# Attention and FFN on one core: v with keys on partitions, and a 32-bit path through TensorE transposes for the first four attention jobs

## The chip, the core and the metric

The kernel runs on one core of one Trainium2 chip. The time is the device time of one launch in microseconds (us). A profile is one execution of the same program under the hardware profiler.

The engines are called as in the profile: PE is TensorE's matrix product and PEld its weight load, DVE is VectorE, ACT is ScalarE, POOL is GpSimd and SP is SyncE, which here only issues transfers. ACT issues some transfers too (ACTq in the profile).

## The reference

There are 8 batches of 8 heads, 576 positions and a head dimension of 64. The attention is causal, with a bias from running sums of a per-position value; its output, with the heads side by side, goes through a feed-forward network (FFN) with a piecewise activation.

```python
scores = scale * np.matmul(q, k.transpose(0, 1, 3, 2))
cum = np.cumsum(np.maximum(s, 0.0), axis=-1)
bias = -(cum[:, :, :, None] - cum[:, :, None, :])
scores = np.where(causal, -1000000000.0, scores + np.minimum(bias, 0.0))
attn = np.exp(scores - np.max(scores, axis=-1, keepdims=True))
attn = attn / (np.sum(attn, axis=-1, keepdims=True) + 1e-09)
out = np.matmul(attn, v)                       # 8 x 8 x 576 x 64
x = out.transpose(0, 2, 1, 3).reshape(8 * 576, 512)
h = x @ w_in                                   # 512 x 2048
g = np.where(h >= 1, h, np.where(h <= -1, 0.0, (h + 1) ** 2 / 4))
result = g @ w_out                             # 2048 x 512
```

q, k, v and s are 32-bit floating point; w_in and w_out come in 64 bits.

## The kernel before

**Split numbers.** Large products run in 16-bit floats on TensorE, but each operand is held as a high half and a low half (the rest after rounding), each scaled by a power of two or by a bound of the largest value. A product of two such operands takes three TensorE passes: high by high, low by high and high by low.

**Attention jobs.** A job is a pair of heads (n, from 0 to 31) and a half of the queries (hf). The first half has 320 queries in three tiles of 64, 128 and 128; the second has 256 in two tiles. The list `jobs` (L492) runs through the first halves of a batch's four pairs, then through its second halves. A job has eight slots (`att_slot`, L494): slot 0 loads the running sums' rows, slots 2 to 7 issue one unit of scores each, slot 3 loads the next job's q and k, and slot 7 issues the attention product of the job before.

For a unit, `scores` (L393) multiplies q by k on PE (L408 in 32 bits for the first twelve jobs, later L411 and L412), adds the mask and takes the row minimum of the negated scores on DVE (L417), and takes the exponential with its row sums on ACT (L428). When both heads of a tile are done, `weights_t` (L434) makes the weights: DVE forms 1/sum (L444, L445), POOL writes the first head's high half (L449), ACT scales the second head in place (L450), POOL writes that one's high and low half (L451, L452), and DVE writes the first head's low half (L455, in `rest`). Then SP transposes the tile by DMA (L456) from `pb` into `pt`, since the product needs the keys on partitions. `att_out` (L463) runs the three-pass product of `pt` and `vt` on PE (L474), 18 instructions for a first half and 30 for a second, and writes x in two halves on ACT (L485) and DVE (L486).

**v.** `load_v` (L253) brings a batch's v, transposed on the host, with the two heads' dimensions on partitions and 576 keys along the row. `batch_v` and `batch_scales_v` (L258, L267) take its largest value for every partition (L262), a power of two for each, and one maximum over all partitions by a PE transpose and a spread (`column_max`, L107, and `spread`, L117). `v_prep` (L365) clears the pad (L371) and writes the high half on POOL (L372); for the first four pairs POOL also scales v and writes the low half (L374, L375), for the others DVE writes it in `v_turn` (L382). `v_turn` then transposes the tile by DMA (L384).

**Weights.** The first stage of the program decodes w_in from 64-bit words in 16 chunks of 128 x 512, four to each of the first four jobs: ACT takes absolute values (L200) and, for every second chunk, decodes a low part (L207); DVE takes the chunk's peak (L201) and joins the bits (L202, L208, or L210 and L211). After all chunks `w1.scale` (L213) forms the bound of the weight: a maximum over the peaks (L216), a PE transpose of it (L107), small DVE steps, a spread through PE (L117), and the reciprocal (L223, L224). With it, `split` (L226) writes the halves: ACT the high half (L229), and DVE (L237) or POOL (L232, L235) the low half. The transfers of w_out also wait for that bound. The second stage decodes and splits w_out in the same way, between the first FFN steps.

**FFN.** For each 128 of the 2048 inner columns, `ffn_h` (L521) runs twelve products (L528), and ACT and DVE form the activation (L540, L543, L544); ACT and POOL split it (L554, L555), and `ffn_y` (L559) multiplies by w_out (L567). Each batch's halves are 16 such steps. The first half of the first batch runs all its `ffn_h` before its `ffn_y`, since w_out isn't ready.

**Order.** The code issues instructions in program order under a planner that simulates a time line and puts each engine's instructions in an order by it; a `tc.high_priority(offset=...)` block moves its instructions ahead by the offset, and `tc.issue_after` holds one behind another. On the chip each engine's queue runs in the order written. The first stage reads:

```python
load_v(0)
batch_start(0)
for j in range(NPAIR):
    for k in range(8):
        if k % 2 == 0:
            c = 4 * j + k // 2
            w1.decode(c)
            w1.load(c + 3)
        att_slot(j, k)
while late:
    late.pop(0)()
w1.scale(0, LEAST_A)
```

Of the kernel before, what the change touches and what calls it, by code (L numbers as in the profile page):

```python
# [27 lines left out]
SP = NB * P  # L28

# [18 lines left out]
W2_LEAD = 6000  # L48

# [10 lines left out]
F32_JOBS = 12  # L60
V_POOL = 4
# [12 lines left out]
def attention_ffn(ctx: ExitStack, tc: tile.TileContext, qT, kT, vT, s, w_in, w_out, yT):  # L74
# [183 lines left out]
    def batch_v(b):  # L258
        c = csc[b] = ap.tile([P, NPAIR], F32, tag="csc", name=f"c{b}")
        r = rcs[b] = ap.tile([P, NPAIR], F32, tag="rcs", name=f"rc{b}")  # L260
        for p in range(NPAIR):
            V.tensor_reduce(c[:, p:p + 1], vraw[b, p], axis=AX, op=ALU.max, apply_absolute_value=True)  # L262
        pow2floor(c, c, TINY)
        V.reciprocal(r, c)
        V.tensor_scalar(r, r, 4096.0, None, ALU.mult)
# [99 lines left out]
    def v_prep(n):  # L365

        b, p = n // NPAIR, n % NPAIR
        v = vraw.pop((b, p))
        r = rcs[b][:, p:p + 1]
        VB = ap.tile([P, 2, SP], F16, tag="vb", bufs=1, name=f"vb{n}")  # L370
        G.memset(VB[:, :, S:], 0.0)  # L371
        G.tensor_scalar(VB[:, 0, :S], v, r, 1.0, ALU.mult, ALU.mult)  # L372
        if n < V_POOL:
            G.tensor_scalar(v, v, r, 1.0, ALU.mult, ALU.mult)  # L374
            G.tensor_tensor(VB[:, 1, :S], v, VB[:, 0, :S], ALU.subtract)  # L375
        vbs[n] = VB, v, r

    def v_turn(n):
        VB, v, r = vbs.pop(n)
        if n >= V_POOL:  # L380
            with tc.issue_after(ttr[0]):
                V.scalar_tensor_tensor(VB[:, 1, :S], v, r, VB[:, 0, :S], ALU.mult, ALU.subtract)  # L382
        VT = vts[n] = ap.tile([P, 2 * NB, P], F16, tag="vt", bufs=5, name=f"vt{n}")
        nc.sync.dma_start_transpose(out=VT, in_=VB.rearrange("p l n -> p (l n)"))  # L384

# [47 lines left out]

    def weights_t(n, i):  # L434
# [3 lines left out]
        h_off, N, tiles = HALF[hf]  # L438
        if i == tiles[0]:
# [23 lines left out]
    def att_out(n, hf):  # L463
# [19 lines left out]
        e = exs[b][:, p:p + 1]  # L483
# [10 lines left out]
    def att_slot(j, k):  # L494

        if j < len(jobs):
# [11 lines left out]
            if k == 1 and j % (2 * NPAIR) == V_J and j // (2 * NPAIR) + 1 < B:  # L508
# [101 lines left out]
    batch_scales(0)  # L610
# [77 lines left out]
```

## Time and profile before

| | |
|---|---|
| time, median of 3 runs | 1112.76 us (1111.5 to 1112.82) |
| time of the profiled execution | 1112.3 us |
| its span, first to last instruction | 1110.2 us |
| mean granted PE clock | 0.982 |
| bytes moved by DMA | 153.70 MB |
| DMA transposes `pt` and `vt` | 160 and 32 |

The page cuts the span into 40 slices and shows for each engine the busy share in tenths. A table of stretches gives, for each stretch, the microseconds that each engine was busy, the number of its instructions, the granted PE clock (1.00 is full), the share of time in which the DMA engines were busy, and GB/s. A group line reads: line of the kernel, engine, operation, output and input, shape, count, then busy time in us and the mean of one in ns, then the idle time before the group's instructions and what ended it. A line of one source line gives minimum, median and maximum ns, and the first and last start.

### The profile page before, as it was taken

How to read it: one execution, taken by the hardware profiler on the slowest of the kernel's cores; microseconds unless marked ns; L12 is line 12 of the kernel's file. 1: busy time of each engine (PE TensorE's matmuls, PEld its weight loads, DVE VectorE, ACT ScalarE, POOL GpSimd, SP SyncE). 2: the span in 40 equal slices, each digit the busy share in tenths (PEclk: the TensorE clock that was granted, in tenths of full speed). 3: DMA queues.
4: the chain of work that ended last, by engine and by line, in shares of the span. 5: the costliest groups of instructions: out<-in, count | busy, mean ns of one | idle time of the engine just before them, and what ended most of it. 6: DMA issues, size and time to landing. Idle time of an engine off the chain costs nothing.

```text
span 1110.2 us, 25043 instructions
## 1 busy us (share of the span) xinstructions
PE 999.0 (90%) x8470; PEld 771.2 (69%) x8470; DVE 855.0 (77%) x2392; ACT 715.9 (64%) x1683; POOL 657.2 (59%) x1161
## 2 busy tenths in 40 slices
PE   0454799899999999999999999999999999899998
PEld 0132466588767877777777877787777877787787
DVE  7979987578868877878787877787777886887533
ACT  3647766467557775777567775877576755777432
POOL 3666275676647664766566755766476665765522
PEclk9997899699999999999999999999999999999999
DMA  8984536767638763987558763977387874666300
GB/s 257 241 174 129 186 78 126 140 120 152 127 84 187 165 151 72 181 164 158 106 119 186 156 149 74 193 155 167 68 178 155 170 129 80 152 156 138 68 24 20
DMA packets 339623, 153.70 MB, mean 138 GB/s; under 512 B 290728, under 2 KB 321320, under 8 KB 339496
## 3 DMA queue, kind: packets, MB, share of 16 engines
q1 hardware_dynamic: 329792, 142.17, 60.2%
q10 hardware_dynamic: 9704, 9.93, 2.9%
q8 instruction: 67, 1.10, 0.4%
q14 instruction: 60, 0.49, 0.1%
HBM read 71.00 MB, written 9.73 MB: 73 GB/s over the span
## 4 chain that ended last, share of the span: by engine, by line
PE 61%; DVE 15%; DMA 7%; POOL 7%; issue 6%; ACT 4%; ACTq 0%; DVEq 0%; SPq 0%; POOLq 0%
PE h L528 25%; PE y L567 24%; PE px L474 4%; DMA pt<-pb 4%; PE s L411 3%; DVE pb L455 3%; PE s L412 3%; DVE p L417 2%; POOL pb L449 2%; DVE Q1s L362 1%; ACT u L540 1%; PE s L408 1%; DMA wor<-in_moe_w_out_dram 1%; POOL pb L452 1%; DVE h L543 1%
## 5 line engine op out<-in xcount | busy, mean ns | idle before, releaser
L528 PE MATMUL h<-x,WI 128*128 128x256 f16 (+1 forms) x3072 | 463.5, 290 | 22.2 <-DVE u L544 19.6
L567 PE MATMUL y<-g,WO 128*128 128x256 f16 (+1 forms) x3072 | 453.0, 287 | 8.4 <-POOL g L555 6.5
L528 PEld LDWEIGHTS <-WI 128*128 128x128 f16 x3072 | 291.2, 99 | 116.3 <-issue 27.9
L567 PEld LDWEIGHTS <-WO 128*128 128x128 f16 x3072 | 288.1, 98 | 93.4 <-issue 13.8
L555 POOL TENSOR_TENSOR g<-u,g 128x320 f16<-128x320 f32 (+1 forms) x256 | 204.5, 799 | 161.2 <-ACT g L554 156.1
L428 ACT ACTIVATE p<-p,mn 64x64 f32<-64x64 f32 (+4 forms) x320 | 179.5, 561 | 140.2 <-DVE mn L417 123.0
L540 ACT ACTIVATE u<-h,ub,us 128x320 f32<-128x320 f32 (+1 forms) x256 | 149.3, 583 | 121.6 <-PE h L528 119.7
L543 DVE SCALAR_TENSOR_TENSOR h<-h,ws,u 128x320 f32<-128x320 f32 (+1 forms) x256 | 132.4, 517 | 96.9 <-ACT u L540 94.4
L449 POOL TENSOR_SCALAR pb<-p,rs 64x128 f16<-64x128 f32 (+4 forms) x160 | 95.3, 595 | 173.3 <-DVE rs L445 108.0
L452 POOL TENSOR_TENSOR pb<-p,pb 64x128 f16<-64x128 f32 (+4 forms) x160 | 169.1, 1057 | 9.3
L455 DVE SCALAR_TENSOR_TENSOR pb<-p,rs,pb 64x128 f16<-64x128 f32 (+4 forms) x160 | 132.3, 827 | 44.9 <-POOL pb L449 44.7
L417 DVE CUSTOM_DVE_ANT_0 p<-s,mask 64x64 f32<-64x64 f32 (+4 forms) x320 | 134.6, 421 | 33.5 <-PE s L412 17.4
L544 DVE SCALAR_TENSOR_TENSOR u<-u,r,h 128x320 f32<-128x320 f32 (+1 forms) x256 | 130.2, 509 | 6.2
L411 PE MATMUL s<-K1s,Q1s 128*128 128x288 f32 (+4 forms) x312 | 117.5, 378 | 11.4 <-DVE Q1s L362 7.1
L450 ACT ACTIVATE p<-p,rs 64x64 f32<-64x64 f32 (+4 forms) x160 | 89.5, 559 | 58.9 <-DVE rs L445 57.7
L554 ACT CAST g<-u 128x320 f16<-128x320 f32 (+1 forms) x256 | 108.1, 422 | 9.8 <-DVE u L544 9.1
L451 POOL TENSOR_SCALAR pb<-p 64x128 f16<-64x128 f32 (+4 forms) x160 | 93.9, 587 | 11.8 <-ACT p L450 10.0
L412 PE MATMUL s<-K2s,Q2s 68*128 68x288 f32 (+4 forms) x312 | 95.9, 307 | 1.1 <-DMA K2s<-cumd 0.7
L474 PEld LDWEIGHTS <-vt 128*64 128x64 f16 x1536 | 74.0, 115 | 32.9 <-issue 17.9
L474 PE MATMUL px<-pt,vt 128*64 128x256 f16 (+3 forms) x1536 | 84.1, 262 | 10.8 <-DMA pt<-pb 6.8
L411 PEld LDWEIGHTS s<-K1s,Q1s 128*128 128x128 f32 (+1 forms) x312 | 56.6, 181 | 21.2 <-issue 6.7
L363 DVE TENSOR_TENSOR K2s<-rk,K1s 64x1152 fp32r<-64x1152 f32 (+1 forms) x52 | 59.1, 1136 | 2.2 <-ACT K1s L360 0.9
(123 smaller groups left out, 963.3 us busy)
## 6 DMA issues: line engine op xcount, KB each, us to landing
rk<-in_k_dram SPq DMA_DIRECT2D x56, 288.0 KB
v<-in_v_dram SPq DMA_DIRECT2D x32, 288.0 KB
wir<-in_moe_w_in_dram SPq DMA_DIRECT2D x16, 512.0 KB
wor<-in_moe_w_out_dram SPq DMA_DIRECT2D x16, 512.0 KB
rk<-in_k_dram SPq DMA_DIRECT2D x48, 160.0 KB
rq<-in_q_dram SPq DMA_DIRECT2D x48, 160.0 KB
rq<-in_q_dram SPq DMA_DIRECT2D x56, 128.0 KB
out_dram<-o ACTq DMA_DIRECT2D x32, 160.0 KB
```

Source lines behind the costliest of these rows:

```text
L411: T.matmul(sc[:R, :c1 - c0], Q1[:, hd, qo:qo + R], K1[:, hd, c0:c1], start=True, stop=False)
L417: ttr[0] = V.tensor_tensor_reduce(out=Pt[:R, c0:c1], in0=sc[:R, :c1 - c0], in1=mask[:R, mo:mo + c1 - c0], scale=-0.125, scalar=3.0e38 if m ...
L428: A.activation(Pt[:R, :W], Pt[:R, :W], AF.Exp, bias=m2[:R], scale=-1.0, accum_out=sums[n, i][:R, hd:hd + 1])
L452: G.tensor_tensor(los[1], pw, his[1], ALU.subtract)
L455: V.scalar_tensor_tensor(los[0], pv, rs[:R, :1], his[0], ALU.mult, ALU.subtract)
L474: T.matmul(px[hd * D:(hd + 1) * D, lo:N], VT[:, vl * NB + j, hd * D:(hd + 1) * D], PT[:, 4 * j + 2 * hd + pl, lo:], start=(m == 0), stop=( ...
L528: T.matmul(h[:, :N], WI[4 * kt + ft // 4][:, wl, ft % 4 * P:(ft % 4 + 1) * P], x[:, kt, xl], start=(n == 0), stop=(n == 3 * NKT - 1),)
L540: first = A.activation(u, h[:, :N], AF.Relu, bias=ubi[b], scale=usc[b]).ins
L543: V.scalar_tensor_tensor(h[:, :N], h[:, :N], wsc[b], u, ALU.mult, ALU.max)
L544: V.scalar_tensor_tensor(u, u, r, h[:, :N], ALU.min, ALU.mult)
L555: G.tensor_tensor(g[:, 1], u, g[:, 0], ALU.subtract)
L567: T.matmul(ys[b, hf, m][:, :N], WO[8 * (m // 2) + ft // 2][:, wl, c0:c0 + P], g[:, gl], start=(ft == 0 and n == 0), stop=(ft == NFT - 1 an ...
```

## The change

v comes from the host with keys in rows and a pair's two heads side by side; a tile holds 128 keys on partitions and five blocks of keys along the row, the last one half filled and cleared on POOL. So `vt` is written in place by `v_prep` and `v_low`, over 640 columns, and v's DMA transposes go. v has one scale for a batch instead of one for each partition. Each load is two transfers.

The first four jobs (`PLAIN_JOBS`) take another path, `plain_t`: POOL normalizes both heads' weights in place in 32 bits, PE transposes them in blocks of up to 128 keys into the PSUM banks that the FFN's second product uses later, ACT copies them into a 32-bit `pt`, and PE multiplies them by v as loaded, in 32 bits. v's halves for the first four pairs are prepared in jobs 4 and 5, for the second halves of the queries. The next batch's v is loaded one job later in the first batch.

v's load and its scale move into the first job (slots 2 and 6), and `w1.scale` and `batch_scales(0)` get a lead of 6000 in the planner.

```diff
     def load_v(b):
         for p in range(NPAIR):
-            v = vraw[b, p] = ap.tile([P, S], F32, tag="vraw", bufs=4, name=f"v{b}_{p}")
-            nc.sync.dma_start(v, vT[b, p])
+            v = vraw[b, p] = ap.tile([P, NB, P], F32, tag="vraw", bufs=4, name=f"v{b}_{p}")
+            G.memset(v[TAIL:, NB - 1], 0.0)
+            nc.sync.dma_start(v[:, :NB - 1], vn[b, p, :SP - P].rearrange("(j p) n -> p j n", p=P))
+            nc.sync.dma_start(v[:TAIL, NB - 1], vn[b, p, SP - P:])
...
     def v_prep(n):
...
-        VB = ap.tile([P, 2, SP], F16, tag="vb", bufs=1, name=f"vb{n}")
-        G.memset(VB[:, :, S:], 0.0)
-        G.tensor_scalar(VB[:, 0, :S], v, r, 1.0, ALU.mult, ALU.mult)
+        VT = vts[n] = ap.tile([P, 2, NB, P], F16, tag="vt", bufs=5, name=f"vt{n}")
+        G.tensor_scalar(VT[:, 0], v, r, 1.0, ALU.mult, ALU.mult)
         if n < V_POOL:
             G.tensor_scalar(v, v, r, 1.0, ALU.mult, ALU.mult)
-            G.tensor_tensor(VB[:, 1, :S], v, VB[:, 0, :S], ALU.subtract)
+            G.tensor_tensor(VT[:, 1], v, VT[:, 0], ALU.subtract)
...
-        nc.sync.dma_start_transpose(out=VT, in_=VB.rearrange("p l n -> p (l n)"))
...
+    def plain_t(n, i):
...
+        V.tensor_scalar(rs[:R], sums.pop((n, i))[:R], EPS, 2.0 ** -12, ALU.add, ALU.mult)
+        V.reciprocal(rs[:R], rs[:R])
+        for hd, Pt in enumerate(pbs.pop((n, i))):
+            G.tensor_scalar(Pt[:R, :W], Pt[:R, :W], rs[:R, hd:hd + 1], 1.0, ALU.mult, ALU.mult)
+            pp = ps_y.tile([P, 512], F32, tag=f"y{turn[0] % 4}", name=f"pp{n}_{i}_{hd}")
+            turn[0] += 1
+            for j in range(i + 1):
+                T.transpose(pp[:, j * R:(j + 1) * R], Pt[:R, j * P:(j + 1) * P], ident[:R, :R])
+            A.copy(
+                PT[:, hd:2 * (i + 1):2, off - h_off:off - h_off + R],
+                pp[:, :(i + 1) * R].rearrange("p (j r) -> p j r", r=R),
+            )
...
     def att_out(n, hf):
...
+        if plain(n, hf):
+            e = exs[b]
+            for j in range(nj):
+                lo = max(0, j * P - h_off)
+                for hd in range(2):
+                    T.matmul(
+                        px[hd * D:(hd + 1) * D, lo:N], vraw[b, p][:, j, hd * D:(hd + 1) * D],
+                        PT[:, 2 * j + hd, lo:], start=(j == 0), stop=(j == nj - 1),
+                    )
...
-            if k == 1 and hf == 0:
+            if plain(n, 0):
+                if k in (1, 4) and hf == 1 and j < PLAIN_JOBS + 2:
+                    v_prep(2 * (j - PLAIN_JOBS) + k // 4)
+            elif hf == 0 and k == 1:
                 v_prep(n)
-            if k == V_K and hf == 0:
-                v_turn(n)
+            elif hf == 0 and k == V_K:
+                v_low(n)
...
-    load_v(0)
-    batch_start(0)
     for j in range(NPAIR):
         for k in range(8):
...
+            if (j, k) == (0, 2):
+                load_v(0)
+            if (j, k) == (0, 6):
+                batch_start(0)
             att_slot(j, k)
     while late:
         late.pop(0)()
-    w1.scale(0, LEAST_A)
-    batch_scales(0)
+    with tc.high_priority(offset=SCALE_LEAD):
+        w1.scale(0, LEAST_A)
+        batch_scales(0)
```

More of the change, by code (lines that the diff above doesn't have):

```diff
@@ L48 @@
 W2_LEAD = 6000
+SCALE_LEAD = 6000
 G_BUFS = 4
@@ L60 @@
 F32_JOBS = 12
+PLAIN_JOBS = 4
 V_POOL = 4
@@ L73, in attention_ffn @@
 @with_exitstack
-def attention_ffn(ctx: ExitStack, tc: tile.TileContext, qT, kT, vT, s, w_in, w_out, yT):
+def attention_ffn(ctx: ExitStack, tc: tile.TileContext, qT, kT, vn, s, w_in, w_out, yT):
     nc = tc.nc
@@ L315, in whole, with plain @@
         return jobs.index((n, hf)) < F32_JOBS
+    def plain(n, hf):
+        return jobs.index((n, hf)) < PLAIN_JOBS
     def operands(n, hf):
@@ L367, in v_prep, with v_low @@
         b, p = n // NPAIR, n % NPAIR
[L368 to L372 removed]
+        v, r = vraw.pop((b, p)), rcs[b]
+        VT = vts[n] = ap.tile([P, 2, NB, P], F16, tag="vt", bufs=5, name=f"vt{n}")
+        G.tensor_scalar(VT[:, 0], v, r, 1.0, ALU.mult, ALU.mult)
         if n < V_POOL:
             G.tensor_scalar(v, v, r, 1.0, ALU.mult, ALU.mult)
[L375 to L379, printed above, removed]
+            G.tensor_tensor(VT[:, 1], v, VT[:, 0], ALU.subtract)
+        vbs[n] = VT, v, r
+    def v_low(n):
+        VT, v, r = vbs.pop(n)
         if n >= V_POOL:
             with tc.issue_after(ttr[0]):
[L382 to L384 removed]
+                V.scalar_tensor_tensor(VT[:, 1], v, r, VT[:, 0], ALU.mult, ALU.subtract)
     vbs = {}
@@ L432, in scores @@
             weights_t(n, i)
+    def plain_t(n, i):
+        off, R, W = QT[i]
+        h_off, N, tiles = HALF[i // 3]
+        if i == tiles[0]:
+            pts_[n, i // 3] = ap.tile([P, 2 * (tiles[-1] + 1), N], F32, tag="pt", bufs=2, name=f"pt{n}_{i // 3}")
+        PT = pts_[n, i // 3]
+        rs = ap.tile([P, 2], F32, tag="rs", bufs=4, name=f"rs{n}_{i}")
+        V.tensor_scalar(rs[:R], sums.pop((n, i))[:R], EPS, 2.0 ** -12, ALU.add, ALU.mult)
[10 more added lines that the diff above has]
+            )
+    turn = [0]
     def weights_t(n, i):
@@ L438, in weights_t @@
         h_off, N, tiles = HALF[hf]
+        if plain(n, hf):
+            plain_t(n, i)
+            return
         if i == tiles[0]:
@@ L467, in att_out @@
         nj = tiles[-1] + 1
-        PT, VT = pts_.pop((n, hf)), vts[n]
+        PT, e = pts_.pop((n, hf)), 2.0 ** -12
         px = ps_s.tile([P, 512], F32, tag="s", name=f"px{n}_{hf}")
-        steps = [(j, vl, pl) for j in range(nj) for vl, pl in ((0, 0), (1, 0), (0, 1))]
+        if plain(n, hf):
+            e = exs[b]
[6 more added lines that the diff above has]
+                    )
+        steps = [] if plain(n, hf) else [(j, vl, pl) for j in range(nj) for vl, pl in ((0, 0), (1, 0), (0, 1))]
         for m, (j, vl, pl) in enumerate(steps):
@@ L507, in att_slot @@
                 att_load(*jobs[j + 1])
-            if k == 1 and j % (2 * NPAIR) == V_J and j // (2 * NPAIR) + 1 < B:
+            if k == 1 and j % (2 * NPAIR) == V_J + (j < 2 * NPAIR) and j // (2 * NPAIR) + 1 < B:
                 load_v(j // (2 * NPAIR) + 1)
@@ L670 @@
         "in_k_dram": c(inputs["k"].transpose(0, 1, 3, 2)),
-        "in_v_dram": c(inputs["v"].transpose(0, 1, 3, 2)).reshape(B, NPAIR, P, S),
+        "in_v_dram": c(inputs["v"].reshape(B, NPAIR, 2, S, D).transpose(0, 1, 3, 2, 4)).reshape(B, NPAIR, S, P),
         "in_s_dram": c(inputs["s"]).reshape(B * H, S),
```

33 lines of the change are left out of this document (14 added, 19 removed).

## The prediction

> **What bounds the kernel now.** I read the page first, for who is busy when.
>
> ```profile
> span 1110.2 us, 25043 instructions
> PE 999.0 (90%) x8470; PEld 771.2 (69%) x8470; DVE 855.0 (77%) x2392; ACT 715.9 (64%) x1683; POOL 657.2 (59%) x1161
> ...
> PE   0454799899999999999999999999999999899998
> ...
> DVE  7979987578868877878787877787777886887533
> ```
>
> TensorE holds the last six sevenths; before that, VectorE is the full engine. The change works on the beginning, so the table of stretches is cut there: 24.3 is the first score product, 63.8 the end of the last w_in peak, 84.9 the third pair's turn in the first FFN product, 160 the place where TensorE fills.
>
> ```profile
> core 0: us, PE busy (x) PEld busy (x) DVE busy (x) ACT busy (x) POOL busy (x), PEclk, DMA share, GB/s
> 0.00:24.30 24.30, 0.51 (x2) 0.18 (x2) 16.02 (x39) 9.13 (x10) 6.92 (x19) 1.00 0.83 255
> 24.30:63.80 39.50, 17.62 (x55) 9.04 (x54) 36.83 (x112) 24.07 (x58) 27.13 (x49) 1.00 0.99 233
> 63.80:84.90 21.10, 11.44 (x73) 7.54 (x74) 15.79 (x61) 10.23 (x27) 9.97 (x27) 1.00 0.81 180
> 84.90:160.00 75.10, 51.23 (x284) 31.21 (x284) 69.80 (x161) 55.00 (x96) 42.68 (x43) 0.86 0.45 133
> ...
> 210.00:1050.00 840.00, 818.27 (x7257) 645.42 (x7257) 661.81 (x1865) 569.17 (x1383) 525.59 (x954) 1.00 0.67 140
> ```
>
> Up to 160 us VectorE works 138.4 us (the sum of four rows) and is idle 21.6: 8.3, 2.7, 5.3 and 5.3. From 210 to 1050 TensorE is idle only 21.7 of 840. So a microsecond that leaves VectorE's path before 160 moves the end by about one; later it moves nothing. DMA is the second suspect: its share is 0.99 from 24 to 64. The third is a position in a queue:
>
> ```profile
> 63.68 0.15 DVE L216 TENSOR_REDUCE t_wi<-peak_wi 128x1 f32<-128x16 f32 x1
> ...
> 76.50 0.37 PE L107 MATMUL row_wi<-ident,t_wi 128*1 128x128 f32 x1
> ...
> 80.76 0.14 DVE L224 TENSOR_SCALAR r_wi<-r_wi 128x1 f32<-128x1 f32 x1
> ```
>
> The first weight's largest value stands at 63.8, TensorE takes it up at 76.5, and its reciprocal, for which every w_in split waits, is there at 80.9: 17.1 us for about 3 us of small steps.
>
> **VectorE's ledger, the terms of the sum.** Groups of VectorE from 0 to 81 us, then the spread of four of them (minimum/median/maximum ns; L211's rows from the whole span):
>
> ```profile
> L417 DVE CUSTOM_DVE_ANT_0 p<-s,mask 64x64 f32<-64x64 f32 (+2 forms) x24 | 8.3, 345 | 2.6 <-POOL pb L452 1.5 <-PE s L408 1.1
> L202 DVE TENSOR_SCALAR WO<-WO 128x512 int32<-128x512 int32 x16 | 8.0, 501 | 0.1
> L455 DVE SCALAR_TENSOR_TENSOR pb<-p,rs,pb 64x128 f16<-64x128 f32 (+2 forms) x12 | 8.0, 664 | 4.2 <-POOL pb L449 4.2
> L208 DVE SCALAR_TENSOR_TENSOR WO<-wir,WO 128x512 int32<-128x512 int32 x8 | 7.7, 962 | 0.3 <-ACT wir L207 0.3
> L211 DVE SCALAR_TENSOR_TENSOR WO<-wir,WO 128x512 int32<-128x512 int32 x8 | 6.8, 856 | 0.0
> L444 DVE TENSOR_SCALAR rs<-sm 128x2 f32<-128x2 f32 (+1 forms) x12 | 4.3, 360 | 0.4 <-ACT p L428 0.4
> L262 DVE TENSOR_REDUCE c<-v 128x1 f32<-128x576 f32 x4 | 3.0, 750 | 1.3 <-DMA v<-in_v_dram 1.3
> ```
>
> ```profile
> L202 DVE TENSOR_SCALAR WO<-WO x16: 404/414/1292, 8.5 to 63.1; 128x512 int32<-128x512 int32 x16
> L208 DVE SCALAR_TENSOR_TENSOR WO<-wir,WO x8: 659/682/2489, 9.7 to 56.6; 128x512 int32<-128x512 int32 x8
> L211 DVE SCALAR_TENSOR_TENSOR WO<-wir,WO x8: 675/686/1595, 13.4 to 65.4; 128x512 int32<-128x512 int32 x8
> L444 DVE TENSOR_SCALAR rs<-sm x160: 150/169/1111, 30.1 to 1037.4; 128x2 f32<-128x2 f32 x128, 64x2 f32<-64x2 f32 x32
> ```
>
> 1. Four plain jobs have no low half of the weights, so 12 of L455 go: **-8.0** of work, and with them the 4.2 idle that waited on GpSimd's L449: **-4.2**.
> 2. v's four reductions no longer stand first in the queue; the 1.3 us wait for v goes: **-1.3**. They read 640 instead of 576 columns: 3.0 x 64/576 = **+0.3**. The other steps on v's scale are the same small ones in another order: nothing.
> 3. Mean against median of four groups: 16 x 0.087 + 8 x 0.280 + 8 x 0.170 + 12 x 0.191 = 7.3 us by which VectorE's instructions are stretched. I put that down to GpSimd running beside them: it works 44.0 us up to 84.9, so 0.166 per GpSimd microsecond (bounds: nothing, if the cause is another, or all of it). What GpSimd loses and gets:
>
> ```profile
> L452 POOL TENSOR_TENSOR pb<-p,pb 64x128 f16<-64x128 f32 (+2 forms) x12 | 9.5, 788 | 0.4
> L449 POOL TENSOR_SCALAR pb<-p,rs 64x128 f16<-64x128 f32 (+2 forms) x12 | 7.1, 593 | 16.0 <-DMA pt<-pb 4.9 <-DVE rs L444 4.8 <-issue 2.9
> L451 POOL TENSOR_SCALAR pb<-p 64x128 f16<-64x128 f32 (+2 forms) x12 | 6.6, 549 | 0.7 <-ACT p L450 0.7
> L375 POOL TENSOR_TENSOR vb<-v,vb 128x576 f16<-128x576 f32 x4 | 5.4, 1351 | 0.1
> L372 POOL TENSOR_SCALAR vb<-v,rc 128x576 f16<-128x576 f32 x4 | 4.0, 1004 | 16.7 <-DVE rc L265 16.7
> L374 POOL TENSOR_SCALAR v<-v,rc 128x576 f32<-128x576 f32 x4 | 3.0, 738 | 0.1
> ```
>
> L449, L451 and L452 go for 12 tiles: 23.2. v's preparation (L372, L374, L375, 12.4) moves to jobs 4 and 5, behind 84.9. Added are 24 normalizations f32 to f32 of 64, 192 and 320 columns. By L374 (738 ns for 576 columns) they cost 8 x 0.74 = 5.9, by L449's mean 24 x 0.593 = 14.2; I take 8, since L374 has the same types. GpSimd falls by 27.6 us, and VectorE's stretch by 27.6 x 0.166 = **-4.6**.
> 4. The moved 12.4, at 640 columns 13.8, now lies in the stretch from 84.9 to 160, where VectorE is 93% busy: 13.8 x 0.166 = **+2.3** (bounds 0 and 13.8, each GpSimd microsecond stopping VectorE wholly).
>
> Work: -8.0 + 0.3 - 4.6 + 2.3 = -10.0. Idle: -5.5. Together **-15.5**.
>
> The largest row bears on a rule. L208's worst took 2489 ns against 682. The Trainium skill, SBUF — State Buffer, section Who interferes with whom, says that VectorE and GpSimd share one pair of ports, held for a whole instruction, so that the second of two such instructions waits fully. The 2489 ns agrees; by that rule the moved preparation could cost its full length, and that is rival D.
>
> **What is added elsewhere and why it stays covered.**
>
> ```profile
> L408 PE MATMUL s<-K2w,Q2w 68*64 68x64 f32 (+2 forms) x24 | 10.8, 573 | 14.0 <-DVE mn L417 11.3 <-issue 2.6
> ...
> L107 PE MATMUL row_m<-ident,mt x8: 270/273/372, 23.0 to 917.0; 128*1 128x128 f32 x8
> ...
> L408 PEld LDWEIGHTS s<-K2w,Q2w x72: 132/192/338, 35.2 to 242.4; 68*128 68x128 f32 x56, 68*64 68x64 f32 x16
> ...
> L428 ACT ACTIVATE p<-p,mn 64x64 f32<-64x64 f32 (+2 forms) x24 | 10.8, 449 | 11.4 <-DVE mn L417 5.8 <-DVE rs L445 4.8 <-POOL p L403 0.7
> L450 ACT ACTIVATE p<-p,rs 64x64 f32<-64x64 f32 (+2 forms) x12 | 5.3, 442 | 4.8 <-DVE rs L445 4.8
> ```
>
> TensorE gets 48 transposes of 128 columns in 32 bits (2, 4 and 6 per job for the three tiles). By L107 alone each costs 0.27, by L107 plus a 32-bit weight load up to 0.27 + 0.34: 13 to 29 us; I take 16, since loads overlap products. The product in 32 bits has 6 instructions instead of 18; between nothing and +2 us per job, I take nothing. TensorE then works some 46 of the first 85 us instead of 29.6, covered while VectorE is the fuller. ACT gets 24 copies out of PSUM of 64 to 384 columns, 24 x 0.45 = 10.8 by L428 and L450, and loses L450's 5.3: 49 of 85.
>
> The DMA queues lose in this part 12 transposes of weights and 4 of v (by their shapes 2.9 + 1.3 = 4.2 MB; the first three stretches moved 19.2 MB, so a fifth). SP carries no transposes any more that hold back w_in loads. v's rows become 512 bytes long in two transfers each, which may cost more than now; the freed fifth covers that. I count nothing for DMA, up or down; what it could give is rival C. The later 28 transposes of v lie where TensorE sets the time: nothing.
>
> The bound's lead brings splits and w_out loads nearer to 64 us. I don't count it on top: VectorE must still do its ledger before 160; the lead is what lets it do so without the idle time of item 1 coming back as a wait for the bound. Late next is then the last job's tail and ACT's splits, which before stood behind 80.9.
>
> The profiled execution took 1112.3 us, 2.1 outside its span: 1112.3 - 15.5 = 1096.8. The median of the three runs is 0.5 higher, so I say **1097**.
>
> **The rivals.** About 0.2%, 2.2 us, is what a measurement of this kernel can tell from no change.
>
> - **B, work without idle.** The 5.5 us of waits return in another form (a product waits for its copy, the bound's small steps wait in VectorE's queue). For it: every hop through TensorE and ACT is in order. Then -10.0, 1103; without relief from GpSimd (item 3 at nothing) -8.0 + 0.3 + 2.3 = -5.4, 1107.
> - **C, DMA was the limit too.** For it: share 0.99. The early idle of 8.3 loses 3 more, TensorE's 21.7 later loses a fifth, 4, as v's transposes leave SP's queue: -22.5, 1090. Against: VectorE was 93% busy in that very stretch.
> - **D, the moved v preparation stops VectorE for its full 13.8** instead of 2.3: 11.5 more, 1109. Against: the mean stretch is a sixth of GpSimd's time.
> - **E, slower: transposes serialize the attention.** TensorE's queue is in order; if each tile's transposes stand ahead of the next tile's scores, a tile costs its whole chain: two scores 1.15, mask and minimum 0.35, exponential 0.45 and its sum, rs 0.36, two normalizations 0.67, four transposes 1.1, a copy 0.45: 4.6, and with three hops that wait behind a 0.5 us VectorE instruction 6.1. Twelve tiles: 73 us from 24.3, and 3 for the last product, so the FFN begins at 100 instead of 84.9: +15, 1128. It decides from 5.0 us per tile, where 24.3 + 60 + 3 passes 84.9 by 2.2. Against: two score buffers and four p buffers let the next scores go ahead. The Trainium skill, TensorE: Matmul & The Clock Gate, Part 4, adds that transposes don't count as activity for the clock, so that TensorE might run slow there; here the granted clock is 1.00 in all stretches to 84.9 and no row shows a run of transposes.
> - **F, no change.** The copies stand in ACT's queue ahead of w_in's first decode step, and each of 16 chunks starts 1 us later (a transpose group, 1.1): 16 us, which cancels the gain: 1112.
>
> **How the numbers follow.** A, the forecast, 0.46 (own range 1092 to 1102); B 0.18; C 0.14; D 0.06; F 0.06; E 0.10. Faster is A to D, 0.84; same 0.06; slower 0.10. The range leaves out F and E and reaches from C with a margin, 1087, to D, 1109.
>
> **What would show it.** VectorE's busy time up to the filling of TensorE near 128 us; L455 absent before the fifth job; r_wi within 5 us of t_wi; the FFN's first product near 70; TensorE full from about 145, and the stretch of 840 us as long as now. Wrong, if r_wi comes early but TensorE fills at 155 or later (B, D or F: look for waits on transposes in ACT and for stretched L202 behind 84.9), if the scores of job 3 end later than now (E), or if the later stretch shortens by over 3 us (C).

## The result and the profile after

The changed kernel takes **1120.14 us** (median of seven runs, 1115.6 to 1121.97) against 1112.76 (seven runs, 1109.08 to 1115.96): ratio 1.0059, 95% interval 1.0034 to 1.0084, so slower by some 7 us. The prediction was 1097. The profiled execution took 1121.97 us.

The page of the changed kernel, in the lines that stand ahead of the prediction for the kernel before:

```profile
span 1120.2 us, 24958 instructions
...
PE 1018.8 (91%) x8494; PEld 777.5 (69%) x8494; DVE 844.7 (75%) x2364; ACT 716.5 (64%) x1695; POOL 676.0 (60%) x1149
...
PE   2584699899999999899999999999999999999998
...
DVE  6759897678777877787778877887778877887533
```

The table of stretches of the changed kernel, cut at the same times as before:

```profile
core 0: us, PE busy (x) PEld busy (x) DVE busy (x) ACT busy (x) POOL busy (x), PEclk, DMA share, GB/s
0.00:24.30 24.30, 3.41 (x10) 1.83 (x10) 18.13 (x48) 10.02 (x17) 7.91 (x23) 1.00 0.82 231
24.30:63.80 39.50, 24.09 (x71) 12.84 (x73) 28.96 (x96) 23.61 (x59) 16.01 (x37) 1.00 0.71 177
63.80:84.90 21.10, 18.98 (x77) 10.74 (x74) 9.04 (x46) 13.03 (x34) 9.82 (x24) 0.68 0.38 115
84.90:160.00 75.10, 47.07 (x248) 28.51 (x248) 69.35 (x154) 49.86 (x86) 37.84 (x42) 0.77 0.43 125
...
210.00:1050.00 840.00, 816.36 (x7208) 640.26 (x7205) 656.34 (x1855) 567.70 (x1384) 551.39 (x952) 0.99 0.62 129
```

VectorE works 125.5 us up to 160 (four rows) instead of 138.4. Only part of these 13 us is work that left: at 160 the changed kernel is also less far (12 steps of u done, 15 in the kernel before). Up to 84.9 VectorE is idle for 28.8 us (6.2, 10.5 and 12.1) instead of 16.3. In 63.8 to 84.9, TensorE is the full engine: 19.0 of 21.1 us.

Where VectorE's idle time ends, from the waits of the changed kernel between 24 and 85 us (waiting engine and line, releaser, us in total, times, longest):

```profile
ACT WO L203 <- DMA wir<-in_moe_w_in_dram: 12.9, 8, 2.8
...
POOL v L377 <- PE px L502: 10.0, 3, 4.8
DVE WO L204 <- ACT WO L203: 9.8, 7, 2.3
...
DVE top_wi L112 <- PE row_wi L110: 3.7, 1, 3.7
...
DVE bound_wi L121 <- PE col_wi L120: 1.5, 1, 1.5
```

Up to 63.8 us VectorE now waits for w_in (9.8 of 10.5 us idle: DMA, then ACT). Of the 12.1 after that, 5.2 are waits for the bound by name; the rest are short waits for the attention's own steps, while the splits that could fill them stand behind the bound. The bound in the time line of the changed kernel (start, us, engine, line, operation):

```profile
59.73 0.15 DVE L219 TENSOR_REDUCE t_wi<-peak_wi 128x1 f32<-128x16 f32 x1
...
71.79 1.33 PE L502 MATMUL px<-pt,v 128*64 128x320 f32 x4 [0.58 <-DVE mn L418]
...
74.65 0.74 PE L502 MATMUL px<-pt,v 128*64 128x192 f32 x3
...
75.33 0.37 PE L110 MATMUL row_wi<-ident,t_wi 128*1 128x128 f32 x1
...
79.53 0.14 DVE L227 TENSOR_SCALAR r_wi<-r_wi 128x1 f32<-128x1 f32 x1
```

The last peak comes 4 us earlier than before, its reciprocal only 1.2: `row_wi` stands directly behind the third job's product, 15.6 us after what it needs (start to start). Both write a bank of the same ring of two, `ps_s`, in which the scores, the products and the small results of `column_max` and `spread` take turns in program order. A lead in the planner can't move an instruction past the users of its bank.

To place a difference in time I compare the start of the same matrix product in two traces: the 7700th from the end, at 217.6 us in the kernel before. The changed kernel reaches it 5.1 us later, and takes 4.9 us more from there to the end. Up to this product, before and changed (columns as in the table of stretches):

```profile
0.00:217.60 217.60, 131.90 (x770) 83.07 (x772) 177.56 (x503) 129.93 (x265) 121.48 (x199) 0.91 0.67 167
0.00:222.70 222.70, 149.36 (x792) 91.65 (x794) 171.35 (x487) 131.37 (x277) 112.80 (x192) 0.85 0.56 142
```

For the same progress VectorE works 6.2 us less and is idle 11.3 us more (51.4 instead of 40.0). So two things went wrong: the idle time took more than the work gave, and the later stretch, which should have stayed as long as it was, grew.

### The profile page after: what moved, and what is told of

It is laid out like the page before. It is cut to its first block, busy times and chain, and to the rows that moved or that the text cites. A ratio compares the mean times of both kernels' runs of the same rounds, so it can differ in the third digit from the quotient of the medians.

```text
span 1120.2 us, 24958 instructions
## 1 busy us (share of the span) xinstructions
PE 1018.8 (91%) x8494; PEld 777.5 (69%) x8494; DVE 844.7 (75%) x2364; ACT 716.5 (64%) x1695; POOL 676.0 (60%) x1149
## 5 line engine op out<-in xcount | busy, mean ns | idle before, releaser
L562 PE MATMUL h<-x,WI 128*128 128x256 f16 (+1 forms) x3072 | 456.8, 290 | 25.5 <-DVE u L578 20.4
L601 PEld LDWEIGHTS <-WO 128*128 128x128 f16 x3072 | 288.7, 98 | 91.7 <-issue 12.5
L589 POOL TENSOR_TENSOR g<-u,g 128x320 f16<-128x320 f32 (+1 forms) x256 | 219.2, 856 | 200.6 <-ACT g L588 197.7
L476 POOL TENSOR_SCALAR pb<-p,rs 128x256 f16<-128x256 f32 (+4 forms) x148 | 93.0, 629 | 134.0 <-DVE rs L472 47.9
L479 POOL TENSOR_TENSOR pb<-p,pb 128x256 f16<-128x256 f32 (+4 forms) x148 | 156.3, 1058 | 8.2
L482 DVE SCALAR_TENSOR_TENSOR pb<-p,rs,pb 128x256 f16<-128x256 f32 (+4 forms) x148 | 124.3, 840 | 20.6 <-POOL pb L476 20.4
L477 ACT ACTIVATE p<-p,rs 128x192 f32<-128x192 f32 (+4 forms) x148 | 83.6, 569 | 54.9 <-DVE rs L472 54.5
L478 POOL TENSOR_SCALAR pb<-p 128x256 f16<-128x256 f32 (+4 forms) x148 | 92.6, 627 | 5.1 <-ACT p L477 2.5
L510 PEld LDWEIGHTS <-vt 128*64 128x64 f16 x1464 | 68.1, 112 | 19.5 <-issue 13.5
L510 PE MATMUL px<-pt,vt 128*64 128x256 f16 (+3 forms) x1464 | 77.2, 257 | 1.4 <-DMA pt<-pb 1.3
```

The costliest lines, as they stand in the source:

```text
L479: G.tensor_tensor(los[1], pw, his[1], ALU.subtract)
L482: V.scalar_tensor_tensor(los[0], pv, rs[:R, :1], his[0], ALU.mult, ALU.subtract)
L510: T.matmul(px[hd * D:(hd + 1) * D, lo:N], vts[n][:, vl, j, hd * D:(hd + 1) * D], PT[:, 4 * j + 2 * hd + pl, lo:], start=(m == 0), stop=(m ...
L562: T.matmul(h[:, :N], WI[4 * kt + ft // 4][:, wl, ft % 4 * P:(ft % 4 + 1) * P], x[:, kt, xl], start=(n == 0), stop=(n == 3 * NKT - 1),)
L589: G.tensor_tensor(g[:, 1], u, g[:, 0], ALU.subtract)
L601: T.matmul(ys[b, hf, m][:, :N], WO[8 * (m // 2) + ft // 2][:, wl, c0:c0 + P], g[:, gl], start=(ft == 0 and n == 0), stop=(ft == NFT - 1 an ...
```

## Experiments

All times are medians; the kernel before, on the same chips, took 1111.6 to 1113.8. "At 218" and "later" are the two parts of the difference in the profiles, as above.

| kernel | us (range) | ratio, 95% interval | at 218 | later |
|---|---|---|---|---|
| changed | 1120.1 (1115.6 to 1122.0) | 1.0059 (1.0034 to 1.0084) | +5.1 | +4.9 |
| e1 v by keys alone | 1120.3 (1119.0 to 1123.3) | 1.0077 (1.0057 to 1.0096) | +6.5 | +0.6 |
| e2 changed, no lead | 1120.7 (1117.3 to 1123.1) | 1.0073 (1.0052 to 1.0095) | +2.2 | +4.6 |
| e3 changed, bound in own bank | 1113.9 (1110.3 to 1117.2) | 1.0015 (0.9998 to 1.0032) | -3.2 | +3.6 |
| e4 changed, v's low halves on VectorE | 1120.2 (1115.4 to 1121.7) | 1.0066 (1.0044 to 1.0088) | +3.0 | +5.6 |
| e6 before, bound led, own bank | 1120.7 (1117.2 to 1126.2) | 1.0074 (1.0046 to 1.0101) | +5.2 | +4.4 |
| e7 e3 and maxima apart | 1107.2 (1106.1 to 1109.0) | 0.9950 (0.9931 to 0.9970) | -1.9 | -2.4 |
| e8 changed, maxima apart | 1107.7 (1106.1 to 1108.3) | 0.9949 (0.9930 to 0.9968) | -3.3 | -2.3 |
| e9 e1 and GpSimd spaced | 1108.9 (1106.6 to 1111.2) | 0.9954 (0.9935 to 0.9973) | +0.5 | -2.3 |
| e10 e9 and maxima apart | 1096.5 (1095.5 to 1099.0) | 0.9848 (0.9832 to 0.9865) | -2.1 | -13.0 |
| e11 changed, GpSimd spaced | 1116.3 (1106.3 to 1120.1) | 1.0000 (0.9971 to 1.0029) | -2.5 | -0.5 |
| e12 changed, both | 1095.9 (1090.8 to 1105.8) | 0.9854 (0.9815 to 0.9893) | -5.9 | -14.5 |
| e13 before, maxima apart | 1126.2 (1121.5 to 1129.7) | 1.0109 (1.0084 to 1.0133) | +0.6 | +15.6 |
| e16 e12, bound in own bank | 1094.8 (1094.4 to 1095.4) | 0.9837 (0.9824 to 0.9850) | -2.3 | -14.3 |
| e17 e12, no lead | 1102.5 (1092.2 to 1105.3) | 0.9881 (0.9847 to 0.9915) | +3.6 | -12.6 |
| e18 changed, plain matmuls for transposes | 1122.3 (1119.5 to 1123.6) | 1.0098 (1.0080 to 1.0116) | +1.9 | +9.0 |
| e19 e16, the same | 1095.5 (1093.2 to 1099.5) | 0.9863 (0.9839 to 0.9887) | -3.8 | -11.3 |

The first theory was that the score banks hold the bound back and VectorE idles for it. Its rivals were that the new layout of v costs by itself, and that GpSimd's preparation of v is in the way. In the texts on record the bank theory is Theory A, from the second set on Theory 1; there Theory 2 is that of v's maxima and Theory 3 that of GpSimd's queue. In e1 and e4 Theory 1 is another: that GpSimd's preparation of v meets the splits of w_in. "Both repairs" are the two edits of e8 and e9.

**e1, v by keys alone.** No plain jobs, no lead, v loaded and scaled first as before.

```diff
-PLAIN_JOBS = 4
+PLAIN_JOBS = 0
-SCALE_LEAD = 6000
+SCALE_LEAD = 0
...
     att_load(0, 0)
+    load_v(0)
+    batch_start(0)
```

> Only the v layout of the change (keys on partitions, no DMA transposes of v, one scale for a batch); v is loaded and scaled first as before, no plain jobs, no lead for the first weight's bound. Theory 1 (the loss is made between 80 and 98 us, where GpSimd's v preparation and the w_in splits meet): nothing of that meets here, so 0.995 to 1.001 of before, and the x of the fourth pair not later than before's 91.3 us. Theory 2 (the v layout itself costs, 512-byte rows, 640 columns, one more job before v is loaded): 1.004 to 1.007, as the whole change.

Measured 1120.3: the layout alone costs as much as the whole change. The first theory can't explain that, since here nothing was meant to lead. The reason shows in GpSimd's rows on `vt` of this kernel:

```profile
L375 POOL TENSOR_SCALAR vt<-v,rc x4: 802/1124/1247, 24.0 to 27.1; 128x640 f16<-128x640 f32 x4
L378 POOL TENSOR_TENSOR vt<-v,vt x4: 1386/1387/1392, 32.9 to 39.5; 128x640 f16<-128x640 f32 x4
```

All four pairs are prepared between 24 and 41 us, ahead of and between the first weights. The old `vb` had one buffer, so each preparation waited for the one before it to be transposed; that wait was a brake that kept GpSimd's queue free for the weights, and the five buffers of `vt` took it away. The first x comes at 62.9 instead of 57.3 us.

**e2, no lead; e3, another bank; e4, v's low halves on VectorE.**

```diff
-SCALE_LEAD = 6000
+SCALE_LEAD = 0
```

> The whole change, but the first weight's bound has no lead in the planner. Theory A (the lead does nothing, since the transpose of the peaks takes its PSUM bank in turn behind the third job's product): the same time as the change, 1.004 to 1.008 of before, and the reciprocal again at 79 to 81 us. Theory B (the lead moves the bound as meant and something else loses): 3 to 8 us slower than the change, reciprocal at 84 us or later.

```diff
+    def own_bank(name, tile_name):
+        if name == "wi0":
+            return ps_h.tile([P, 512], F32, tag="h", name=tile_name)
+        return ps_s.tile([P, 512], F32, tag="s", name=tile_name)
+
     def column_max(src, name):
-        row = ps_s.tile([P, 512], F32, tag="s", name=f"row_{name}")
+        row = own_bank(name, f"row_{name}")
...
-        col = ps_s.tile([P, 512], F32, tag="s", name=f"col_{name}")
+        col = own_bank(name, f"col_{name}")
```

> The whole change, but the first weight's two small TensorE steps use a PSUM bank of the FFN's first product, which is free until then, in place of a score bank. Theory A (the score banks hold the bound back): row_wi by 63 us instead of 75.3, the reciprocal by 68 instead of 79.7, the splits beside the third and fourth job, and the end 5 to 12 us earlier than the change's, 0.993 to 1.001 of before. Theory B (the tail of the fourth job on a slow TensorE sets the start of the FFN in any case): the reciprocal early, but the time within 2 us of the change's.

```diff
-V_POOL = 4
+V_POOL = 0
...
-                    v_prep(2 * (j - PLAIN_JOBS) + k // 4)
+                    m = 2 * (j - PLAIN_JOBS) + k // 4
+                    v_prep(m)
+                    v_low(m)
```

> The whole change, but the low half of v of the first four pairs is written by VectorE after the score step, as for all other pairs, not by GpSimd in place. This takes 8 GpSimd instructions of 0.8 and 1.4 us away and adds 4 of 0.9 us to VectorE. Theory 1 (GpSimd's v preparation stretches VectorE's w_in splits and holds GpSimd's own splits back until the fourth product has read v): the splits take about 0.75 us each again and x of the fourth pair comes at 92 instead of 97.6; 1.000 to 1.003 of before. Rival (GpSimd is innocent; the splits come late for TensorE's sake): 1.004 to 1.008, x at 96 us or later.

The lead brings nothing in time (1120.7 without it; the reciprocal came at 76.6 us, not at the 79 to 81 expected). Taking the low halves from GpSimd brings nothing either (1120.2), though VectorE's splits of w_in then take 959 ns on average instead of 1168 and the fourth pair's x comes at 92.5 us instead of 97.6, as its theory expected. The bank does what the lead was for. The reciprocal's row in e3, and the same stretches:

```profile
L232 DVE TENSOR_SCALAR r_wi<-r_wi x1: 143/143/143, 65.8 to 65.8; 128x1 f32<-128x1 f32 x1
```

```profile
63.80:84.90 21.10, 13.87 (x55) 8.46 (x54) 19.26 (x56) 19.49 (x43) 13.81 (x25) 0.78 0.33 112
84.90:160.00 75.10, 55.73 (x300) 33.86 (x299) 63.64 (x158) 45.47 (x82) 40.71 (x48) 0.79 0.47 134
```

The reciprocal comes at 65.8 instead of 79.5, and VectorE works 19.3 us in 63.8 to 84.9 instead of 9.0. The kernel reaches the mark 8.3 us earlier than the changed one, and its time is 6.3 lower. So the position held the reciprocal back as read. What that costs is less sure, since by the same bank e7 gains only 0.5 us on e8, and e16 only 1 us on e12; the fourth pair's x then comes later (100.1 against 97.6), since the splits now go ahead of the last jobs.

**e6, the bound led in the kernel before** (the edit of e3 and a lead of 6000).

> The kernel before, unchanged in v and in its first four jobs, with the first weight's bound led by 6000 and its two small TensorE results in an h bank instead of a score bank. Theory 1 (the score banks hold the bound back, and VectorE's idle time up to 85 us waits for it): the factor r_wi, at 80.8 us in the kernel before, comes before 70; VectorE stood idle for 2.7 us in 24.3 to 63.8 and 5.3 us in 63.8 to 84.9, and up to those 5 us come back: 1107 to 1110 against 1112.6. Rival (VectorE's work sets the fill, and it is not one instruction shorter here; the last pairs' attention comes later by what the early splits take): 1111 to 1115. If the time goes above 1115, leading the bound costs more than it brings.

Slower by 7 us: `r_wi` comes at 72.9 instead of 80.8, but the fourth pair's x at 105.9 instead of 91.3. An early bound by itself is no gain; I read it as taking VectorE from the attention that the same FFN step needs, which no run separates.

**e7 and e8, maxima apart.** TensorE's longest waits between 210 and 1050, first of the kernel before, then of the changed one:

```profile
PE s L411 <- DVE Q1s L362: 7.1, 7, 1.6
PE y L567 <- POOL g L555: 6.5, 7, 1.3
PE s L411 <- DVE mn L417: 3.8, 5, 1.0
```

```profile
PE h L562 <- DVE u L578: 7.7, 9, 1.3
PE s L412 <- DVE mn L418: 6.7, 11, 1.3
PE y L601 <- POOL g L589: 4.8, 6, 0.8
PE s L412 <- DVE Q1s L367: 2.6, 7, 0.4
```

The wait of h for u is new; the wait for Q1s shrank, so that TensorE's whole idle time there grew by 1.9 us only (21.7 to 23.6). The new wait stands once a batch behind v's four maxima, in the changed kernel's time line:

```profile
427.25 2.99 DVE L267 TENSOR_REDUCE c<-v 128x1 f32<-128x640 f32 x4
430.16 0.53 DVE L578 SCALAR_TENSOR_TENSOR u<-u,r,h 128x320 f32<-128x320 f32 x1
```

Here u waits for 3 us of maxima, and TensorE for u. The kernel before had the same four back to back (0.74 each) with u ahead of them, and no such wait. But e1 has 6.6 us of this wait, and its later part is only 0.6 longer. The edit puts one maximum behind each score step:

```diff
+            if 2 <= k < 5 and j % (2 * NPAIR) == 2 * NPAIR - 1 and j + 1 < len(jobs):
+                with tc.issue_after(ttr[0]):
+                    v_max(jobs[j + 1][0] // NPAIR, k - 2)
             if k == 5 and j + 1 < len(jobs) and jobs[j + 1][0] % NPAIR == 0 and jobs[j + 1][1] == 0:
```

> The changed kernel with the bound's results in an h bank (1113.9 by itself) and, from the second batch on, the four absolute maxima of v put behind one score step each instead of back to back. Theory 2 (the four maxima of 0.80 us stop VectorE for 3 us once a batch, TensorE waits 1.3 us for u each time, 7.7 us in all from 210 to 1050): those waits go, and 3 to 6 us of the time with them, 1108 to 1111. Rival (TensorE's waits for VectorE only move to another place: before has 21 us of them in the same stretch, after 22.7): 1112 to 1115.5.

> The changed kernel with nothing but the maxima put apart. Theory 2: 1114.5 to 1117.5 against 1120.1, and the wait of h for u is under 2 us in 210 to 1050 (7.7 now). Rival (the waits only move): 1118.5 to 1121, with as much waiting under other names.

TensorE's waits in e8 over the same time:

```profile
PE s L420 <- DVE mn L426: 5.8, 10, 1.0
PE y L612 <- POOL g L600: 4.9, 6, 0.8
...
PE h L573 <- DVE u L589: 0.8, 2, 0.4
```

The wait goes (7.7 to 0.8) and the later part falls by 7.2 us, from +4.9 to -2.3: so much the edit is worth there. That the wait alone made the +4.9 is not shown. The time fell by 12.4, and each of e8's six times lies below every one of the changed kernel. The other part lies before 218 us, where e8 is 8.4 us ahead. Up to 160 us all queues of the two kernels have the same order, and still the 401st matrix product starts at 153.1 us instead of 159.5: 6.4 of the 8.4 us aren't made by any queue's order. With the bank (e7) the time is the same as without, so the 6 us of e3 don't add.

**e9, v by keys alone with GpSimd spaced.** Each preparation stands behind the weights before it.

```diff
-        G.tensor_tensor(los[1], pw, his[1], ALU.subtract)
+        last_pool[0] = G.tensor_tensor(los[1], pw, his[1], ALU.subtract).ins
...
+        with tc.issue_after(last_pool[0]) if last_pool[0] is not None else nullcontext():
+            G.tensor_scalar(VT[:, 0], v, r, 1.0, ALU.mult, ALU.mult)
```

> v by keys alone (1120.3), with each pair's preparation on GpSimd put behind the weights of the attention before it, as the kernel before had it by its one vb buffer. Theory 3 (with five vt buffers in place of one vb, all four preparations, 12 instructions and 13.8 us, run between 24 and 41 us, ahead of the first weights; the first x comes 5.6 us later, the bound 2.7 us later and batch 0's second half 6 us later): most of these 6 us come back, 1114.5 to 1117; what is left above the kernel before is the maxima's part. Rival (the layout costs by its 640 columns, its loads and its shared scale, wherever they stand): 1119 to 1121.5.

```profile
L378 POOL TENSOR_SCALAR vt<-v,rc x4: 794/800/967, 23.7 to 68.2; 128x640 f16<-128x640 f32 x4
```

The four now start between 23.7 and 68.2 us instead of 24.0 and 27.1, and the time falls by 11.4 us to 4.6 below the kernel before; 6.0 of it before the mark. The layout itself is a gain, once the brake is back.

**e10 to e13, the two repairs together and apart.** In e11 and e12 the plain path's normalization (L446) sets `last_pool` too, so that in the first batch no preparation runs before the last weights of job 3.

> v by keys alone with both repairs: GpSimd's preparation behind the weights before it (1108.9 by itself) and the maxima of later batches one score step apart. If the two repairs mend two different things (the first stage, and TensorE's waits for u in the batches after, 3.3 us of which are left with the first repair): 1104 to 1107. If they mend the same thing (each brought some 12 us from the same 1120): 1108 to 1110.

> The changed kernel with nothing but GpSimd's preparation of v put behind the weights before it, so that in the first batch none of it runs before the last weights of job 3 are normalized (in the changed kernel it ran at 32.8 to 36.0, 49.0 to 53.6, 65.9 to 68.9, 75.5 to 79.1 and 84.3 to 87.0 us, between the weights and the splits). Theory 3 (that work stands in GpSimd's queue ahead of weights and splits): 1111 to 1116 against 1120.1, and the time at 218 us falls by 4 us or more. Rival (GpSimd had room there, and the preparation now falls between 75 and 160 us, beside VectorE's full queue): 1118 to 1123.

> The changed kernel with both repairs (maxima apart: 1107.7 by itself). If they are two things: 1102 to 1106. If GpSimd's preparation was no cost in this kernel: 1106.5 to 1109. Against the kernel of v by keys alone with both repairs it also shows what the plain 32-bit jobs bring: nothing if the two are within 2 us.

> The kernel before with nothing but its maxima of later batches put one score step apart. Theory 2 (the waits of h for u come with the changed kernel's order; in the kernel before the same four maxima, 0.74 us each and back to back, end in no such wait): no gain, 1111 to 1115 against 1113. Rival (back-to-back maxima cost some 7 us in whichever kernel): 1105 to 1109.

Both repairs give 1096.5 without the plain jobs and 1095.9 with them: the repairs are two things, and the plain 32-bit jobs bring nothing that these runs can tell (0.6 us, and a wider range of times). In e11, GpSimd's wait of 10 us for the product, whose v it scales in place, is gone, and the mark comes 7.6 us earlier than in the changed kernel, but that profile is one of its lower times: its twelve times fall at 1106.3 to 1108.8 (five) and 1115.7 to 1120.1 (seven), so alone it is worth 4 us at the median.

e13 refutes the plain form of the maxima theory. In the kernel before, the same edit costs 12 us, all in the later stretch. The stretches from 210 to 1050 of e10 and e13:

```profile
210.00:1050.00 840.00, 829.78 (x7369) 653.97 (x7368) 672.04 (x1858) 568.61 (x1388) 533.51 (x951) 1.00 0.61 128
```

```profile
210.00:1050.00 840.00, 810.30 (x7105) 636.93 (x7103) 667.62 (x1851) 564.84 (x1371) 529.78 (x947) 0.99 0.66 138
```

TensorE is idle for 10.2 us in e10 and 29.7 in e13 (23.6 in the changed kernel, 21.7 before). In e13 the longest wait is

```profile
PE s L419 <- DVE mn L425: 13.9, 7, 3.2
```

At 592 us VectorE stands at a low half of weights (L463) that waits for GpSimd's L457; the next job's operands and mask are queued behind it; VectorE waits 3.5 us and TensorE 3.2. Just behind it the granted clock reads 0.51 (595.1 to 598.5), and such a fall of 3.4 us comes five times in e13's later part, in the kernel before not once; TensorE's products there are busy for 874.5 us instead of 867.1, about half of the 15.6. So the edit moves not only the maxima: the planner orders all later queues anew, and what waits behind what decides between -14 and +16 us. Which neighbour makes each of those 30 us I haven't separated.

**e14 and e15, the changed kernel again.**

> The changed kernel once more, for a second profile: its times fall into two groups (1115.6 to 1116.8 and 1120.1 to 1122.0), and its profile is of the upper one. The instructions up to 160 us stand in the same order as in the changed kernel with its maxima apart, whose profile reached the last peak of w_in 4.2 us earlier (55.5 against 59.7 us), opened TensorE's clock 5 us earlier and stood 8.4 us ahead at 218 us. If the groups part in the first stage (the landing of w_in, then the clock): a time under 1117 goes with the last peak before 57 and with at most +1 against the kernel before at 218 us, a time over 1120 with 58.5 or later. If they part later: the same first stage, within 1 us, and the difference after 218 us.

> A third profile of the changed kernel, with the same expectation: a time under 1117 with the last peak of w_in before 57 us, over 1120 with 58.5 us or later, and some 5 us between them at 218 us.

Both took over 1121 (1121.25, 1121.58): +4.0 and +5.2 at 218, +5.3 and +4.4 later, with the last peak at 58.6 and 58.3 us. Three profiles agree, then; no profile of the lower times came, and the question of where they part stays open.

**e16 and e17, bank and lead in the repaired kernel.**

> The changed kernel with both repairs (1095.9) and the bound's results in an h bank. If the score bank was a cost of its own in this kernel: 1088 to 1093. If what the bank brought (6 us without the repairs, 0.5 us with the maxima apart) came from the order of later work: 1094 to 1099. If the early bound puts the splits ahead of the last pairs' attention, as it did in the kernel before (x of the fourth pair 14.6 us later): 1099 to 1104.

> The changed kernel with both repairs and no lead for the bound. If the lead does nothing, as in the changed kernel itself (1120.7 without it, 1120.1 with it): 1094 to 1098 against 1095.9. If it is worth what the profiles of the first stage hint at (r_wi 17.3 to 19.8 us after the last peak with it, 21.2 without): 1098 to 1101.

The own bank leaves the median (1094.8 against 1095.9) and makes the times close (1094.4 to 1095.4). Without the lead the ranges overlap with e12's; the profiles differ by 9.5 us at the mark, the medians by 6.6: a hint, no more. e16 is the version to keep: 1.6% below the kernel before.

**e18 and e19, plain matmuls for the transposes.**

```diff
-                T.transpose(pp[:, j * R:(j + 1) * R], Pt[:R, j * P:(j + 1) * P], ident[:R, :R])
+                T.matmul(pp[:, j * R:(j + 1) * R], Pt[:R, j * P:(j + 1) * P], ident[:R, :R], start=True, stop=True)
```

> The changed kernel with its transposes of weights made as plain 32-bit matmuls against the identity (the same result, no transpose instruction). In three profiles of the changed kernel TensorE's clock first rose at 66.4 to 84.7 us, though it was busy for 62% of 25 to 65 us and 89% of 65 to 85 us, nearly half of that with transposes of 0.37 to 0.48 us (0.27 to 0.33 where the clock was up). If transposes don't count as activity for the clock: the first rise comes before 55 us, r_wi before 74 us (78.4 to 79.7 in three profiles) and the time falls to 1112 to 1117. If they count like any matmul (the gaps between keep the clock down): the first rise stays at 62 to 85 us, and the time within 1118 to 1123.

> The same exchange in the changed kernel with both repairs and the bound in its own bank (1094.8). If the clock rises earlier for it, and TensorE's share of the first stage sets the end there: 1088 to 1092. If the clock stays, or VectorE sets the end: 1093 to 1097.

The transposes of the changed kernel from 20 to 62 us, and those of e8 from 62 to 72 us, when its clock was up (minimum/median/maximum ns):

```profile
L450 PE MATMUL pp<-ident,p x25: 311/421/476, 24.1 to 61.9; 128*128 128x128 f32 x20, 64*128 64x64 f32 x5
```

```profile
L458 PE MATMUL pp<-ident,p x18: 221/273/331, 62.2 to 71.9; 128*128 128x128 f32 x16, 64*128 64x64 f32 x2
```

421 against 273 ns: the changed kernel transposed at the low clock before its first record. In e18 the clock's first rise is recorded at 43.0 us, against 67.3, 66.4 and 84.7 in the three profiles of the changed kernel; in e19 at 58.0 against 72.6 in e16. The Trainium skill, TensorE: Matmul & The Clock Gate, Part 4: PE-mode transpose, says that the full clock doesn't engage for transposes, which don't count as busy in the same way; these first rises agree. A plain product stands in the trace as two instructions (96 instead of 48), so TensorE was busier too, 11.6 us instead of 9.5 between 24 and 43; but e8 was busy for 12.5 there, with transposes, and rose at 62.1. The time doesn't fall: `r_wi` comes at 76.9, 2.6 us earlier, still behind the third product; at the mark e18 is 3.2 us ahead of the changed kernel, and its later stretch, ordered anew, takes that back (+9.0). The expected 1112 to 1117 was wrong, and so was e19's 1088 to 1092: the clock is a cost in the first stage, but not what the time hung on.

## Why the prediction was wrong, point by point

- **Work, items 1 to 3: right in size, one term by luck.** The twelve low halves left with their 8.0. The relief was 5.4 instead of 4.6, by the groups of the changed kernel from 0 to 81 us (mean ns is the second number behind the bar):

```profile
L205 DVE TENSOR_SCALAR WO<-WO 128x512 int32<-128x512 int32 x16 | 7.2, 453 | 0.0
L214 DVE SCALAR_TENSOR_TENSOR WO<-wir,WO 128x512 int32<-128x512 int32 x8 | 6.5, 812 | 0.0
...
L211 DVE SCALAR_TENSOR_TENSOR WO<-wir,WO 128x512 int32<-128x512 int32 x8 | 5.4, 678 | 0.0
L267 DVE TENSOR_REDUCE c<-v 128x1 f32<-128x640 f32 x4 | 3.3, 814 | 2.1 <-DMA v<-in_v_dram 2.0
L443 DVE TENSOR_SCALAR rs<-sm 128x2 f32<-128x2 f32 (+1 forms) x12 | 2.3, 195 | 2.2 <-ACT p L429 2.2
```

  16 x 0.048 + 8 x 0.284 + 8 x 0.044 + 12 x 0.165 = 5.4; with the maxima's +0.3 and the 8.0 that is 13.1, where 12.3 was forecast. But GpSimd's work up to 84.9 fell by 10.3 us (44.0 to 33.7) and not by 27.6: its normalizations took 12.7 instead of 8, and the preparation stayed. By 0.166 per GpSimd microsecond that gives 1.7, so 5.4 came near 4.6 by luck, and its cause isn't shown.
- **Idle time, items 1 and 2: the step that failed.** -5.5 was forecast, +12.5 up to 84.9 came, +11.3 up to the mark. The wait on GpSimd's L449 went, and behind it stood w_in's arrival (9.8) and the bound (5.2 by name). "The lead is what lets it do so without the idle time coming back" was wrong because I read the position of `row_wi` as one in a queue that a priority can change; it is one in a ring of two banks (e2, e3). r_wi came 19.8 us behind t_wi, where within 5 was forecast. At 84.9 VectorE had done 12.5 us less, and 13.1 had left: about even, so nothing was gained. What share of the missing 23 us this step has isn't shown: the bank alone brought 6.3 (e3), and next to nothing beside the maxima's edit (e7).
- **Item 4: false in its place, and too small.** The preparation wasn't moved behind 84.9. The program has it in jobs 4 and 5, but nothing held it there: the planner ran it from 32.8 to 87 us, and its in-place scaling (L377) waited 10.0 us for the plain product that reads the same v, at the head of GpSimd's queue. From 84.9 to the mark VectorE works 115.2 us instead of 108.9, which is the 5.1 us of loss and more. The longest item is its low halves of w_in, now beside GpSimd's preparation and splits; before and changed:

```profile
L237 DVE SCALAR_TENSOR_TENSOR WI<-WO,r_wi,WI x11: 734/743/752, 81.7 to 88.9; 128x512 f16<-128x512 f32 x11
L240 DVE SCALAR_TENSOR_TENSOR WI<-WO,r_wi,WI x11: 740/1110/1683, 82.7 to 96.2; 128x512 f16<-128x512 f32 x11
```

  Their mean is 1168 instead of 743 ns, 4.7 us in all, where item 4 had 2.3. Yet where it is less (959 ns in e4, 748 in e18), the mark comes only 2.1 and 3.2 us earlier, and the time stays.
- **TensorE's cover: right in sum, wrong in place.** 46.5 us up to 84.9, as forecast (46): the transposes took 13.5 instead of 16, and the four 32-bit products 4.3 more (10.9 instead of 6.6), where nothing was taken; each has 12 instructions in the trace, not 6. But it is the fuller engine from 63.8 on, and it ran at the low clock there.
- **"The stretch of 840 us as long as now": wrong by 4.4 to 5.3 us** in three profiles. Steps on VectorE that cost 0.3 us more were counted at nothing there, since VectorE isn't the bound; but four of them in a row stand ahead of u, for which TensorE waits, and putting them apart takes 7.2 us off (e8). From the mark to the end TensorE's idle time grew by 2.6 us (25.5 to 28.1) and its busy time by 2.3 (867.1 to 869.4); what made these stays open, as e1 has nearly the same wait and +0.6.
- **Rivals.** B is nearest: idle time returned, through the bound's small steps and the copies' hops, but 18 us of it (from -5.5 to +12.5) and not 5.5, and the time is 23 us above the forecast instead of 6. C: DMA's share fell from 0.99 to 0.71 in 24 to 64 us and VectorE waited for w_in all the same; what then limits those loads wasn't tried. D: a stretch came, 4.7 us and not 13.8; that it set the time, e4 speaks against. E forecast slower, and slower it was, by another way: its condition, scores of job 3 later than now, didn't hold (72.0 against 74.4 us).

The first stage's saving isn't all explained: e8 and the changed kernel have one order up to 160 us and are 6.4 us apart by then. The clock, up from 62.1 to 72.3 us in e8 and for 3.4 us before 84 in the changed kernel, and the last peak, 4.2 us earlier, go with it; that they cause it was not shown.

## What to carry to other kernels

Before counting on a lead, ask for each instruction which buffer it writes and who used that buffer last: a ring in program order outranked the planner's lead here (e2, e3). A wait on a single buffer can be a brake that keeps an in-order queue free; where a change removes it, say what holds the released work back. And after an edit compare the long stretch too: a step on an engine that is not the bound still delays what is queued behind it, here by some 7 us over six batches (e8).

## What the runs showed of the hardware

The granted clock reads 1.00 where the trace has no record yet. The prediction took that for full speed; the durations say otherwise (421 against 273 ns for the same transpose), in the kernel before as well, whose `row_m` took 372 ns at first and 270 later. Before its first record a clock is read from the same instruction at two times.
